# First stage of a transformer-block kernel: tokens, modulation quarters and weight rows issued in another order

## The chip, the cores and the metric

The kernel runs on one core of a Trainium2 chip. The metric is device time in microseconds (us); before the change it was 843.18 us (median of three runs, 842.88 to 844.29). The granted TensorE clock was 0.998 to 1.00 in every run and every run was fast (none showed the lower clock and longer time that mark a slow run).

## The reference, cut to what matters

```python
mod = (silu(c) @ w_mod)                    # six rows of 1024: sa, ca, ga, sb, cb, gb
h = layernorm(x) * (1 + ca) + sa           # x: 2048 tokens x 1024
x = x + ga * linear_attention(h, wqkv, wo) # 32 heads, phi(t) = elu(t) + 1
h = layernorm(x) * (1 + cb) + sb
x = x + gb * (gelu(h @ w_gate) * (h @ w_up)) @ w_down   # 3584 wide
```

The first stage computes, for four blocks of 128 tokens (each called a token below, first to fourth), `h` and the products K = h @ wk and V = h @ wv. K sums over eight blocks `dc` of 128 rows of `wk`. The modulation `1 + ca`, `sa` comes in four quarters `q`: quarter q serves the K rows dc = 2q and 2q+1. So K rows can start as soon as their quarter and their weights are there.

## The kernel before: the parts that matter

Loads go out on one queue (`Q`, the SyncE queue) in this order:

```python
sch.dma(Q, ... C8[:], c_v)                 # c, eight rows, 2 KB
x_dma(0, 1); x_dma(1, 2); wmq_dma(0, (1,)) # tokens 1, 2; half of quarter 0
x_dma(2, 3); wmq_dma(0, (0,)); x_dma(3, 4)
w_dma(WK, ..., 0, 2)                       # wk rows dc 0,1
for q in range(1, 4):
    wmq_dma(q)                             # quarter q, two loads of 512 KB
    w_dma(WK, ..., 2 * q, 2 * q + 2)       # wk rows dc 2q, 2q+1, 512 KB
w_dma(WV, ..., 0, 512)                     # wv, left half of its columns, 1 MB
w_dma(WV, ..., 512, 1024)
```

In the timelines of this stage each engine starts its instructions in the order of the program, so the order of the lines below matters. `warm(n)` issues n filler matmuls, whose results nobody reads, to keep TensorE busy. `ln1_bn`, `ln1_fin`, `xhat_dve` are the layer norm on VectorE (DVE); `t1` transposes a token on TensorE and copies it out on ScalarE (ACT); `mod_cols` makes the columns of a quarter on TensorE, `mod_copy` and `mod1` apply them on DVE; `k_part(q, tokens)` are the K matmuls of quarter q. Seven of the eight K results (4 tokens x 2 halves) stay in seven banks of PSUM (the memory that TensorE writes its results to) through all quarters; the eighth needs bank 4, which holds the modulation columns, so it can only run after the last quarter.

```python
warm(12, 7)
ln1_bn(0, 0); ln1_bn(0, 1); ln1_fin(0); ln1_bn(1, 0); xhat_dve(0, ...); t1(0, 5)
warm(7, 7)
ln1_bn(1, 1); ln1_fin(1); ln1_bn(2, 0); xhat_dve(1, ...); t1(1, 6)
warm(1, 7); mod_cols(0, 4, False); warm(6, 7)
ln1_bn(2, 1); ln1_fin(2); ln1_bn(3, 0); xhat_dve(2, ...)
mod_copy(0, 4); mod1(0, 2, 0, 2); t1(2, 7)
ln1_bn(3, 1); ln1_fin(3); mod1(2, 1, 0, 2)
k_part(0, [0, 1]); xhat_dve(3, ...); k_part(0, [2]); t1(3, 7)
mod_cols(1, 4); mod1(0, 3, 2, 4); mod1(3, 1, 0, 4)
warm(3); k_part(1, [0, 1, 2])
mod_cols(2, 4); mod1(0, 4, 4, 6)
k_part(0, [3]); k_part(1, [3]); warm(1)
k_part(2, [0, 1, 2])                       # "third rows of K"
mod_cols(3, 4); mod1(0, 4, 6, 8)
k_part(2, [3]); warm(2)
k_part(3, [0, 1, 2, 3])                    # for dc: for bank
... k_evac of seven banks ...
kv_mm(3, "k", 1, 4, list(range(NDC)))      # the eighth result, all eight rows
k_evac(3, 1, 4)
for c_ in range(4):
    for jg in range(2):                    # left half of wv, then right half
        kv_mm(c_, "v", jg, nb(), ...); v_evac(...)
    ...
```

Of the kernel before, what the change touches and what calls it, by code (L numbers as in the profile page):

```python
# [12 lines left out]
D = 1024  # L13
# [4 lines left out]
NDC = D // P  # L18
# [27 lines left out]
OFF_WK = OFF_WD  # L46
OFF_WV = OFF_WD + 16384
# [167 lines left out]
def bass_adaLN_cond__linear_attn_block__geglu_ffn__prompt_kernel(  # L215
# [15 lines left out]
    with ExitStack() as es:  # L231
# [79 lines left out]
        def r_sm(name):  # L311
            return [(SMO[name], SMO[name] + SMSZ[name], name)]
# [78 lines left out]
        sch = Sched()  # L391
# [34 lines left out]
            gop(lambda e, k=k: e.memset(bm32f[32 * k:32 * (k + 1), 8 * k:8 * k + 33 * 7 + 1:33], 1.0), wr=r_sm("bm32"))  # L426


        sch.dma(Q, lambda e: e.dma_start(C8[:], c_v), wr=r_sm("c8"), note="c8")

        def x_dma(c0, c1):
            return sch.dma(Q, lambda e: e.dma_start(XALL[:, c0:c1, :], x_v[:, c0:c1, :]), wr=r_xs(c0, c1), note=f"x{c0}")
# [4 lines left out]
        def w_dma(dst, off, name, kind, c0, c1, dc0=0, dc1=NDC):  # L437
            return sch.dma(Q, lambda e: e.dma_start(dst[:, dc0:dc1, c0:c1], wqkv_v[:, dc0:dc1, kind * D + c0:kind * D + c1]),
                           wr=[t_ for dc in range(dc0, dc1) for t_ in r_w(off, name, dc, c0, c1)], note=f"{name}.{dc0}.{c0}")
# [15 lines left out]
        w_dma(WK, OFF_WK, "wk", 1, 0, D, 0, 2)  # L455
        for q in range(1, 4):
            wmq_dma(q)
            w_dma(WK, OFF_WK, "wk", 1, 0, D, 2 * q, 2 * q + 2)
        w_dma(WV, OFF_WV, "wv", 2, 0, 512)
        w_dma(WV, OFF_WV, "wv", 2, 512, 1024)  # L460
        x_dma(4, 8)
        w_dma(WQ, OFF_WQ, "wq", 0, 0, 512)
# [30 lines left out]
        def xhat_dve(c_, dst, rng):  # L493
            sch.op(V, lambda e: e.tensor_scalar(dst[:, :], XALL[:, c_, :], MVA[:, c_, 0:1], RSA[:, c_:c_ + 1],
                                                op0=ALU.subtract, op1=ALU.mult),
                   rd=r_x(c_) + r_smc("mv", c_, 8) + r_smc("rs", c_, 4), wr=rng, note=f"xhat {c_}")
# [5 lines left out]
        def xh_buf(c_):  # L502
            i = c_ % 3
            return XH[i], r_2k(XHO[i], f"xh{i}")
# [10 lines left out]
        def t1(c_, tb):  # L515
            b_, rng = xh_buf(c_)
            sg, ci = divmod(c_, CPG)
            for dc in range(NDC):
                sch.op(T, lambda e, dc=dc: e.transpose(PS16(tb, dc * P, (dc + 1) * P), b_[:, dc * P:(dc + 1) * P], IDENT[:, :]),  # L519
                       rd=rng + r_sm("ident"), pwr=pr(tb), note=f"T1 {c_}.{dc}")  # L520
            sch.op(A, lambda e: e.activation(H1[sg][:, :, ci * P:(ci + 1) * P], PS16(tb).rearrange("p (a b) -> p a b", a=NDC), ACTF.Copy),
                   prd=pr(tb), wr=r_h1(sg, 0, NDC, ci * P, (ci + 1) * P), note=f"h1raw {c_}")
# [26 lines left out]
        def mod1(c0, n, dc0=0, dc1=NDC):  # L549
            sg, ci = divmod(c0, CPG)  # L550
            mods(H1, r_h1, sg, sc1, ci * P, (ci + n) * P, dc0, dc1, "h1")
# [6 lines left out]
        def mod_cols(q, bank, copy=True):  # L558
            o = None
            rng = [(bank * 2048 + q * 16, bank * 2048 + (q + 1) * 16)]  # L560
            for t in range(2):
                for b in range(2):
                    col = q * 4 + t * 2 + b
                    for dc in range(NDC):
                        o = sch.op(T, lambda e, t=t, b=b, dc=dc, col=col: e.matmul(  # L565
                            PS(bank, col, col + 1), WMQ[q][:, dc, t, b * P:(b + 1) * P], SILUT[:, dc:dc + 1],
                            start=(dc == 0), stop=(dc == NDC - 1)),
                            rd=r_wmq(q, t) + r_sm("siluT"), pwr=(rng if dc == 0 else ()), note=f"mod{q}.{t}.{b}.{dc}")
            for t_ in rng:
                sch.ps.set_writer(t_[0], t_[1], o)  # L570
            if copy:
                mod_copy(q, bank)

        def mod_copy(q, bank):
            rng = [(bank * 2048 + q * 16, bank * 2048 + (q + 1) * 16)]
            sch.op(V, lambda e: e.tensor_tensor(MODT[:, q * 4:q * 4 + 4], PS(bank, q * 4, q * 4 + 4), ADD4[:, :], ALU.add),
                   prd=rng, rd=r_sm("add4"), wr=r_smc("modt", q, 16), note=f"modcp{q}")
# [29 lines left out]
        def kv_mm(c_, kind, jg, bank, dcs):  # L607
            sg, ci = divmod(c_, CPG)
            W_, off, name = (WK, OFF_WK, "wk") if kind == "k" else (WV, OFF_WV, "wv")
            o = None  # L610
            for dc in dcs:
                o = sch.op(T, lambda e, dc=dc: e.matmul(PS(bank), H1[sg][:, dc, ci * P:(ci + 1) * P], W_[:, dc, jg * 512:(jg + 1) * 512],  # L612
                                                        start=(dc == 0), stop=(dc == NDC - 1)),
                           rd=r_h1(sg, dc, dc + 1, ci * P, (ci + 1) * P) + r_w(off, name, dc, jg * 512, (jg + 1) * 512),
                           pwr=(pr(bank) if dc == 0 else ()), note=f"{kind} c{c_} jg{jg} dc{dc}")
            if dcs[-1] == NDC - 1:
                pset_writer(bank, o)
# [5 lines left out]
        def v_evac(c_, jg, bank):  # L623
            i = c_ % 3
            sch.op(A, lambda e: e.activation(VS[i][:, jg * 4:jg * 4 + 4, 0:P], PS(bank).rearrange("p (a b) -> p a b", a=4), ACTF.Copy),
                   prd=pr(bank), wr=r_vs(i, jg * 4, jg * 4 + 4, 0, P), note=f"vcp{c_}.{jg}")
# [39 lines left out]
        def warm(n, bank=None):  # L666
            for _ in range(n):
                sch.op(T, lambda e: e.matmul(PS(0 if bank is None else bank), WARM[:, 0:P], WARM[:, :], start=bank is not None,  # L668
                                             stop=bank is not None, skip_group_check=True),
                       rd=R_WARM, pwr=pr(bank) if bank is not None else (), note="warm")  # L670

        def ln1_bn(c_, h):
            src = XALL[:, c_, h * 512:(h + 1) * 512]
            sch.op(V, lambda e: e.bn_stats(STA[:, c_, h * 6:h * 6 + 6], src), rd=r_x(c_, h * 512, h * 512 + 512), wr=r_smc("st", 2 * c_ + h, 24), note=f"bn{h} A{c_}")

        def ln1_fin(c_):
            sch.op(V, lambda e: e.bn_aggr(MVA[:, c_, :], STA[:, c_, :]), rd=r_smc("st", c_, 48), wr=r_smc("mv", c_, 8), note=f"aggr A{c_}")
            sch.op(V, lambda e: e.tensor_scalar(VEA[:, c_:c_ + 1], MVA[:, c_, 1:2], 1e-5, None, op0=ALU.add),
                   rd=r_smc("mv", c_, 8), wr=r_smc("ve", c_, 4), note=f"ve A{c_}")
            sch.op(G, lambda e: e.tensor_tensor(RSA[:, c_:c_ + 1], VEA[:, c_:c_ + 1], NEGHALF[:, :], ALU.pow),  # L680
                   rd=r_smc("ve", c_, 4) + r_sm("neghalf"), wr=r_smc("rs", c_, 4), deps=[last_g[0]], note=f"rstd A{c_}")

        kb0 = {(0, 0): 0, (0, 1): 1, (1, 0): 2, (1, 1): 3, (2, 0): 5, (2, 1): 6, (3, 0): 7}

        def k_part(q, cs):
            for dc in (2 * q, 2 * q + 1):
                for (c_, jg), b in kb0.items():
                    if c_ in cs:
                        kv_mm(c_, "k", jg, b, [dc])


        warm(12, 7)
        ln1_bn(0, 0)
        ln1_bn(0, 1)
        ln1_fin(0)
        ln1_bn(1, 0)
        xhat_dve(0, *xh_buf(0))
        t1(0, 5)
        warm(7, 7)
        ln1_bn(1, 1)  # L700
        ln1_fin(1)
        ln1_bn(2, 0)
        xhat_dve(1, *xh_buf(1))
        t1(1, 6)
        warm(1, 7)
        mod_cols(0, 4, False)
        warm(6, 7)
        ln1_bn(2, 1)
        ln1_fin(2)
        ln1_bn(3, 0)  # L710
        xhat_dve(2, *xh_buf(2))
        mod_copy(0, 4)
        mod1(0, 2, 0, 2)
        t1(2, 7)
        ln1_bn(3, 1)
        ln1_fin(3)
        mod1(2, 1, 0, 2)
        k_part(0, [0, 1])
        xhat_dve(3, *xh_buf(3))
        k_part(0, [2])  # L720
        t1(3, 7)
        mod_cols(1, 4)
        mod1(0, 3, 2, 4)
        mod1(3, 1, 0, 4)
        warm(3)
        k_part(1, [0, 1, 2])
        mod_cols(2, 4)
        mod1(0, 4, 4, 6)
        k_part(0, [3])
        k_part(1, [3])  # L730
        warm(1)
        k_part(2, [0, 1, 2])
        mod_cols(3, 4)
        mod1(0, 4, 6, 8)
        k_part(2, [3])
        warm(2)
        k_part(3, [0, 1, 2, 3])
        for (c_, jg), b in kb0.items():
            k_evac(c_, jg, b)
        kv_mm(3, "k", 1, 4, list(range(NDC)))  # L740
        k_evac(3, 1, 4)
        for c_ in range(4):
            for jg in range(2):
                b = nb()
                kv_mm(c_, "v", jg, b, list(range(NDC)))
                v_evac(c_, jg, b)
            if c_ == 0:
                ln1(4)
                for k, t in enumerate((4, 5, 10, 11)):
                    wm_dma(t, k)  # L750
            if c_ >= 1:
                kvacc(c_ - 1)
            if c_ == 1:
                ln1(5)
            if c_ == 2:
                ln1(6)
                x_dma(12, 16)
                t1d(6)
                t1(4, 4)
                mod1(4, 1)  # L760
# [389 lines left out]
```

## Time and profile before

| | before |
|---|---|
| median, range | 843.18 us, 842.88 to 844.29 (843.33 over six runs) |
| TensorE busy | 830.7 of 841.3 us |
| V starts | 31.40 us |
| first product of K with V starts | 38.56 us |
| first query matmul starts | 47.72 us |
| last landing mark of: first token, first quarter, third rows of wk, right half of wv | 3.90, 10.19, 22.27, 33.29 us |

Lines of the page: busy time per engine, busy share of the 16 DMA engines in 40 slices of 21 us (tenths), the DMA queues, and the chain of waits by engine.

```profile
...
PE 830.7 (99%) x4149; PEld 387.9 (46%) x4229; DVE 492.0 (58%) x883; ACT 294.9 (35%) x483; POOL 24.4 (3%) x64
...
DMA  9991824029778587340555533055553305555000
...
q8 instruction: 34, 0.56, 0.3%
...
PE 96%; DVE 2%; issue 1%; ACT 1%; DMA 0%; ACTq 0%
...
```

TensorE is busy for 99% of the span and holds 96% of the chain. But "busy" counts fillers and modelled ends. Only the first two slices can change, and there the DMA engines are also full ("99"). The useful question is therefore which of the two ended last, stage by stage.

How to read starts. In the timeline the first number is the start, the second the length of the merged group, and the form "128x512" tells its size. A matmul is shown 0.379 us long, but successive 512-wide matmuls start 0.216 us apart, so true idle time on TensorE is start-to-start minus 0.216. L668 is the filler, L565 the quarter columns, L612 K or V, L519 a transpose, L576 the copy of the columns, L538 the modulation. The timeline of before around its last quarter:

```profile
...
24.99 0.94 PE L565 MATMUL ps_all<-siluT,wmq 128*128 128x1 bf16 x32
...
25.79 0.59 PE L612 MATMUL ps_all<-wk,h1T 128*128 128x512 bf16 x2
25.97 0.16 DVE L576 TENSOR_TENSOR modt<-ps_all,add 128x4 f32<-128x4 f32 x1 [3.72 <-PE ps_all L565]
...
26.17 0.73 DVE L538 TENSOR_SCALAR h1T<-h1T,modt 128x512 bf16<-128x512 bf16 x2
26.22 0.59 PE L668 MATMUL ps_all<-warm 128*128 128x512 bf16 x2
...
26.87 4.70 PE L612 MATMUL ps_all<-wk,h1T 128*128 128x512 bf16 x21
...
31.40 2.79 PE L612 MATMUL ps_all<-wv,h1T 128*128 128x512 bf16 x11
...
```

The columns of the last quarter are issued from 24.99 to 25.79 us; the copy and modulation take DVE to 26.58 for the first row; TensorE meanwhile does two K matmuls and two fillers, and goes on at 26.87. V starts at 31.40. 24 useful matmuls take 24 x 0.216 = 5.18 us, but 25.79 to 31.40 is 5.61: 0.43 us are lost here.

The chain of waits of before in order of time (start, length, what) in the middle of the stage:

```profile
...
15.66 0.45 PE ps_all L519 x8
16.11 0.78 PE ps_all L565 x32
16.89 0.08 issue
16.96 0.59 PE ps_all L668 x2
...
17.56 2.76 PE ps_all L612 x12
20.32 0.38 PE ps_all L565 x16
20.70 0.02 issue
20.72 0.55 PE ps_all L565 x16
...
```

Columns of the second quarter at 16.11, fillers, K rows at 17.56; then the columns of the third quarter break at 20.70, where their second half lands (its last mark is 20.67), and the third rows of K start at 22.40, 0.13 us after the last mark of their weights (22.27).

**Landing marks.** A load raises its semaphore (the counter that its users wait on) 16 times; the trace holds the time of each, called a mark here (of c, eight rows, it shows 9). The Trainium skill ("DMA: Bandwidth & Descriptors", "Why a DMA increments its semaphore by 16 and not by 1") says that the engines finish independently and only the full 16 mean that all data has landed. The second load of the third quarter has its fourteenth mark at 19.55 us and its last at 20.67, and the columns went on after the last, at 20.72. In before the first quarter's fourteenth mark is at 9.09 us, its last at 10.19: stragglers of 1.10 us will matter below.

### The profile page before, as it was taken

The numbers are of one execution on the slowest core, as the hardware profiler recorded it, in microseconds if no ns is written. First come the engines' busy times: TensorE is split into PE (matmuls) and PEld (weight loads), VectorE is DVE, ScalarE is ACT, GpSimd is POOL, SyncE is SP. The second block draws the span as 40 slices with busy tenths as digits, with TensorE's granted clock in tenths as the row PEclk, the third lists the DMA queues.
The fourth block names the chain that finished last, engine by engine and source line by source line (L and its number), as shares of the span: only waits on it lengthen the run. The fifth ranks groups of instructions, "written<-read, shape, count | busy, mean of one in ns | idle before, by whom it ended". The sixth has DMA issues, their size and how long they took to land.

```text
span 841.3 us, 11255 instructions
## 1 busy us (share of the span) xinstructions
PE 830.7 (99%) x4149; PEld 387.9 (46%) x4229; DVE 492.0 (58%) x883; ACT 294.9 (35%) x483; POOL 24.4 (3%) x64
## 2 busy tenths in 40 slices
PE   8999999999999999999999999999999999999998
PEld 4454444444444444444444444444444444444445
DVE  5666767867785555654455665346666535655522
ACT  2343333335513344420355442044444104445300
POOL 2000000000200000010000001000000000000000
PEclk9999999999999999999999999999999999999999
DMA  9991824029778587340555533055553305555000
GB/s 286 354 285 26 263 47 105 14 54 233 165 165 252 155 253 206 105 97 23 149 153 154 153 102 69 26 157 150 150 151 101 75 19 158 152 157 141 7 19 26
DMA packets 181750, 112.70 MB, mean 134 GB/s; under 512 B 33080, under 2 KB 172728, under 8 KB 180672
## 3 DMA queue, kind: packets, MB, share of 16 engines
q1 hardware_dynamic: 181696, 111.98, 49.0%
q8 instruction: 34, 0.56, 0.3%
q14 instruction: 20, 0.16, 0.1%
HBM read 100.67 MB, written 4.47 MB: 125 GB/s over the span
## 4 chain that ended last, share of the span: by engine, by line
PE 96%; DVE 2%; issue 1%; ACT 1%; DMA 0%; ACTq 0%
PE ps_all L1006 23%; PE ps_all L1031 23%; PE ps_all L1003 22%; PE ps_all L612 12%; PE ps_all L934 7%; PE ps_all L653 6%; PE ps_all L668 1%; PE ps_all L634 1%; DVE h1T L538 1%; PE ps_all L584 0%; PE ps_all L836 0%; PE ps_all L565 0%; PE ps_all L519 0%; DVE ww L1019 0%; DVE ww L1016 0%
## 5 line engine op out<-in xcount | busy, mean ns | idle before, releaser
L1006 PE MATMUL ps_all<-h2T,wu 128*128 128x512 bf16 x896 | 339.6, 379 | 2.0
L1003 PE MATMUL ps_all<-h2T,wg 128*128 128x512 bf16 x859 | 325.6, 379 | 0.0
L1031 PE MATMUL ps_all<-wd,yT 128*128 128x512 bf16 (+1 forms) x907 | 193.2, 372 | 0.9
L1014 ACT ACTIVATE q<-ps_all 128x512 f32<-128x512 f32 x112 | 66.9, 597 | 229.4 <-PE ps_all L1003 224.5
L1031 PEld LDWEIGHTS ps_all<-wd,yT 128*128 128x128 bf16 x924 | 90.4, 98 | 103.2
L1003 PEld LDWEIGHTS ps_all<-h2T,wg 128*128 128x128 bf16 x896 | 87.7, 98 | 105.8 <-issue 0.2
L1006 PEld LDWEIGHTS ps_all<-h2T,wu 128*128 128x128 bf16 x896 | 87.7, 98 | 105.6
L1016 DVE SCALAR_TENSOR_TENSOR ww<-q,ps_all 128x512 f32<-128x512 f32 x112 | 77.0, 688 | 88.2 <-ACT guh L1015 88.2
L1019 DVE SCALAR_TENSOR_TENSOR ww<-th,guh 128x512 f32<-128x512 f32 x112 | 77.6, 693 | 77.9 <-ACT th L1018 77.9
L1018 ACT ACTIVATE th<-ww 128x512 f32<-128x512 f32 x112 | 70.5, 630 | 85.8 <-DVE ww L1016 85.8
L1021 DVE TENSOR_TENSOR yT<-ww,ps_all 128x512 bf16<-128x512 f32 x112 | 76.9, 687 | 3.8
L1036 DVE TENSOR_TENSOR ps_all<-ps_all,gbb 128x512 f32<-128x512 f32 (+1 forms) x33 | 22.5, 683 | 94.8 <-PE ps_all L1031 94.8
L1015 ACT ACTIVATE guh<-ps_all 128x512 f32<-128x512 f32 x112 | 66.3, 592 | 0.0
L601 ACT ACTIVATE eb<-ps_all 128x512 f32<-128x512 f32 x64 | 37.5, 601 | 77.9 <-PE ps_all L612 37.8
L653 PE MATMUL ps_all<-h1T,wq 128*128 128x512 bf16 x245 | 56.8, 379 | 1.4 <-DVE pq L604 0.7
L612 PE MATMUL ps_all<-wv,h1T 128*128 128x512 bf16 x254 | 57.8, 379 | 0.2
L612 PE MATMUL ps_all<-wk,h1T 128*128 128x512 bf16 x251 | 57.6, 379 | 0.2
L934 PE MATMUL ps_all<-w,pq 128*128 128x512 bf16 x251 | 56.0, 379 | 0.3
L602 DVE TENSOR_SCALAR eb<-eb 128x512 f32<-128x512 f32 x64 | 27.1, 424 | 34.0 <-ACT eb L601 33.6
L934 PEld LDWEIGHTS ps_all<-w,pq 128*128 128x128 bf16 x256 | 25.0, 98 | 30.2 <-issue 0.2
L612 PEld LDWEIGHTS ps_all<-wv,h1T 128*128 128x128 bf16 x256 | 24.9, 98 | 30.0 <-DVE eb L602 0.6
L612 PEld LDWEIGHTS ps_all<-wk,h1T 128*128 128x128 bf16 x256 | 24.6, 98 | 29.8 <-DVE h1T L538 1.5
(81 smaller groups left out, 398.8 us busy)
## 6 DMA issues: line engine op xcount, KB each, us to landing
wg<-in_B_w_gate_dram SPq DMA_DIRECT2D x56, 512.0 KB, 4.1
wu<-in_B_w_up_dram SPq DMA_DIRECT2D x56, 512.0 KB, 5.3
wmst<-in_w_mod_dram SPq DMA_DIRECT2D x8, 1024.0 KB, 11.6
rb<-scr_rd SPq DMA_DIRECT2D x32, 256.0 KB, 6.9
wd<-in_B_w_down_dram SPq DMA_DIRECT2D x7, 1024.0 KB, 7.6
wmq<-in_w_mod_dram SPq DMA_DIRECT2D x8, 512.0 KB, 7.0
out_dram<-xall SPq DMA_DIRECT2D x31, 128.0 KB, 1.7
xall<-in_A_x_dram SPq DMA_DIRECT2D x3, 1024.0 KB, 11.9
```

The lines of the kernel that those rows point to most:

```text
L612: o = sch.op(T, lambda e, dc=dc: e.matmul(PS(bank), H1[sg][:, dc, ci * P:(ci + 1) * P], W_[:, dc, jg * 512:(jg + 1) * 512], start=(dc == 0 ...
L653: o = sch.op(T, lambda e, dc=dc: e.matmul(PS(b), WQ[:, dc, qc * P:(qc + 1) * P], H1[sg][:, dc, :], start=(dc == 0), stop=(dc == NDC - 1)), ...
L934: last[half] = sch.op(T, lambda e, g=g, half=half: e.matmul(PS(b0 + half), PQ[sg][:, g, ci * P:(ci + 1) * P], W2[:, g, half * 512:(half + ...
L1003: og = sch.op(T, lambda e, dc=dc: e.matmul(PS(bg), WG[slot][:, dc, e_ * P:(e_ + 1) * P], H2[sg][:, dc, :], start=(dc == 0), stop=(dc == ND ...
L1006: ou = sch.op(T, lambda e, dc=dc: e.matmul(PS(bu), WU[slot][:, dc, e_ * P:(e_ + 1) * P], H2[sg][:, dc, :], start=(dc == 0), stop=(dc == ND ...
L1014: sch.op(A, lambda e: e.activation(Q1[j][:, :], PS(bg), ACTF.Square, scale=math.sqrt(GELU_A)), prd=pr(bg), wr=rq, note=f"q1 {fc}")
L1015: ogh = sch.op(A, lambda e: e.activation(GUH[j][:, :], PS(bg), ACTF.Copy, scale=0.5), prd=pr(bg), wr=rg, note=f"gh {fc}")
L1016: sch.op(V, lambda e: e.scalar_tensor_tensor(WW[j][:, :], Q1[j][:, :], 1.0, PS(bg), op0=ALU.add, op1=ALU.mult), rd=rq, prd=pr(bg), wr=rw, ...
L1018: sch.op(A, lambda e: e.activation(TH[j][:, :], WW[j][:, :], ACTF.Tanh, scale=GELU_C), rd=rw, wr=rt, note=f"th {fc}")
L1019: sch.op(V, lambda e: e.scalar_tensor_tensor(WW[j][:, :], TH[j][:, :], 1.0, GUH[j][:, :], op0=ALU.add, op1=ALU.mult), rd=rt + rg, wr=rw, n ...
L1021: sch.op(V, lambda e: e.tensor_tensor(YT[:, fc, :], WW[j][:, :], PS(bu), ALU.mult), rd=rw, prd=pr(bu), wr=r_yt(fc), note=f"yT {fc}")
L1031: o = sch.op(T, lambda e, b=b, fc=fc, c0=c0, c1=c1, n=n: e.matmul(PS(b, 0, n), YT[:, fc, ci * P:(ci + 1) * P], WDT[fc // 4][:, fc % 4, c0:c1],
```

## The change

Its intent: start the loads sooner, apply each quarter and token as it arrives, fill the wait at the last quarter, and let V use the left half of its weights for two tokens before the right half is needed.

```diff
-        sch.dma(Q, lambda e: e.dma_start(C8[:], c_v), wr=r_sm("c8"), note="c8")
+        sch.dma(A, lambda e: e.dma_start(C8[:], c_v), wr=r_sm("c8"), note="c8")
 ...     # last wk rows in two loads, left half of wv in two loads
-        w_dma(WV, OFF_WV, "wv", 2, 0, 512)
+            for d0, d1 in ((2 * q, 2 * q + 2),) if q < 3 else ((6, 7), (7, 8)):
+                w_dma(WK, OFF_WK, "wk", 1, 0, D, d0, d1)
+        w_dma(WV, OFF_WV, "wv", 2, 0, 512, 0, 4)
+        w_dma(WV, OFF_WV, "wv", 2, 0, 512, 4, 8)
 ...     # front, as it stands after the change (cut):
+        warm(11, 7)
+        ... t1(0, 5) ... warm(6, 7)
+        mod_cols(0, 4, False)
+        ln1_bn(2, 0); xhat_dve(1, ...); t1(1, 6); ln1_bn(2, 1); ln1_fin(2)
+        mod_copy(0, 4); mod1(0, 1, 0, 2)
+        warm(4, 7); k_part(0, [0])
+        ln1_bn(3, 0); mod1(1, 1, 0, 2); k_part(0, [1])
+        xhat_dve(2, ...); t1(2, 7); ln1_bn(3, 1); ln1_fin(3)
+        mod1(2, 1, 0, 2); warm(5); k_part(0, [2])
+        xhat_dve(3, ...); mod_cols(1, 4); mod1(0, 3, 2, 4); t1(3, 7)
+        k_part(1, [0, 1, 2]); mod1(3, 1, 0, 4); k_part(0, [3])
+        mod_cols(2, 4); mod1(0, 4, 4, 6); k_part(1, [3]); warm(1)
         k_part(2, [0, 1, 2]); mod_cols(3, 4); mod1(0, 4, 6, 8); k_part(2, [3])
-        warm(2)
-        k_part(3, [0, 1, 2, 3])
+        kv_mm(3, "k", 1, 4, list(range(6)))
+        for (c_, jg), b in kb0.items():
+            kv_mm(c_, "k", jg, b, [6, 7])
+        kv_mm(3, "k", 1, 4, [6, 7])
 ...
-            for jg in range(2):
+            for vc, jg in (((0, 0), (1, 0)), ((0, 1), (1, 1)), ((2, 0), (2, 1)), ((3, 0), (3, 1)))[c_]:
```

Four parts: **c** (its load moves to the ScalarE queue), **front** (order up to the last quarter), **tail** (six rows of the eighth result fill the wait), **V** (left half split, V order changed).

More of the change, by code (lines that the diff above doesn't have):

```diff
@@ L457, in bass_adaLN_cond__linear_attn_block__geglu_ffn__prompt_kernel @@
             wmq_dma(q)
-            w_dma(WK, OFF_WK, "wk", 1, 0, D, 2 * q, 2 * q + 2)
-        w_dma(WV, OFF_WV, "wv", 2, 0, 512)
+            for d0, d1 in ((2 * q, 2 * q + 2),) if q < 3 else ((6, 7), (7, 8)):
+                w_dma(WK, OFF_WK, "wk", 1, 0, D, d0, d1)
+        w_dma(WV, OFF_WV, "wv", 2, 0, 512, 0, 4)
+        w_dma(WV, OFF_WV, "wv", 2, 0, 512, 4, 8)
         w_dma(WV, OFF_WV, "wv", 2, 512, 1024)
@@ L683, in bass_adaLN_cond__linear_attn_block__geglu_ffn__prompt_kernel, with k_part @@
         kb0 = {(0, 0): 0, (0, 1): 1, (1, 0): 2, (1, 1): 3, (2, 0): 5, (2, 1): 6, (3, 0): 7}
-        def k_part(q, cs):
-            for dc in (2 * q, 2 * q + 1):
+        def k_part(q, cs, dcs=(0, 1)):
+            for dc in [2 * q + k for k in dcs]:
                 for (c_, jg), b in kb0.items():
@@ L689, in k_part @@
                         kv_mm(c_, "k", jg, b, [dc])
-        warm(12, 7)
+        warm(11, 7)
         ln1_bn(0, 0)
@@ L698, in bass_adaLN_cond__linear_attn_block__geglu_ffn__prompt_kernel @@
         t1(0, 5)
-        warm(7, 7)
         ln1_bn(1, 1)
         ln1_fin(1)
+        warm(6, 7)
+        mod_cols(0, 4, False)
         ln1_bn(2, 0)
@@ L704, in bass_adaLN_cond__linear_attn_block__geglu_ffn__prompt_kernel @@
         t1(1, 6)
-        warm(1, 7)
-        mod_cols(0, 4, False)
-        warm(6, 7)
         ln1_bn(2, 1)
         ln1_fin(2)
+        mod_copy(0, 4)
+        mod1(0, 1, 0, 2)
+        warm(4, 7)
+        k_part(0, [0])
         ln1_bn(3, 0)
+        mod1(1, 1, 0, 2)
+        k_part(0, [1])
         xhat_dve(2, *xh_buf(2))
-        mod_copy(0, 4)
-        mod1(0, 2, 0, 2)
         t1(2, 7)
@@ L717, in bass_adaLN_cond__linear_attn_block__geglu_ffn__prompt_kernel @@
         mod1(2, 1, 0, 2)
-        k_part(0, [0, 1])
+        warm(5)
+        k_part(0, [2])
         xhat_dve(3, *xh_buf(3))
-        k_part(0, [2])
-        t1(3, 7)
         mod_cols(1, 4)
         mod1(0, 3, 2, 4)
+        t1(3, 7)
+        k_part(1, [0, 1, 2])
         mod1(3, 1, 0, 4)
-        warm(3)
-        k_part(1, [0, 1, 2])
+        k_part(0, [3])
         mod_cols(2, 4)
         mod1(0, 4, 4, 6)
-        k_part(0, [3])
         k_part(1, [3])
@@ L735, in bass_adaLN_cond__linear_attn_block__geglu_ffn__prompt_kernel @@
         k_part(2, [3])
-        warm(2)
-        k_part(3, [0, 1, 2, 3])
+        kv_mm(3, "k", 1, 4, list(range(6)))
+        for (c_, jg), b in kb0.items():
+            kv_mm(c_, "k", jg, b, [6, 7])
+        kv_mm(3, "k", 1, 4, [6, 7])
         for (c_, jg), b in kb0.items():
             k_evac(c_, jg, b)
-        kv_mm(3, "k", 1, 4, list(range(NDC)))
         k_evac(3, 1, 4)
         for c_ in range(4):
-            for jg in range(2):
+            for vc, jg in (((0, 0), (1, 0)), ((0, 1), (1, 1)), ((2, 0), (2, 1)), ((3, 0), (3, 1)))[c_]:
                 b = nb()
-                kv_mm(c_, "v", jg, b, list(range(NDC)))
-                v_evac(c_, jg, b)
+                kv_mm(vc, "v", jg, b, list(range(NDC)))
+                v_evac(vc, jg, b)
             if c_ == 0:
```

## The prediction

> **What bounds the kernel.** TensorE. The page shows PE busy 830.7 of 841.3 us and the chain of waits 96% PE, at granted clock 1.00. From about 31 us on matmuls follow one another at 0.216 us in the timeline. The change touches only the first stage, so it can win only what TensorE wastes there. In the timeline the stage runs from 2.2 us to 31.40 us, where the V products start. It holds 64 K matmuls (13.8 us), four token transposes (about 2.2), four modulation quarters (3.2). The rest is filler ("warm") matmuls and short gaps: 12 fillers up to 7.41 us, 7 to 9.70, one at 10.15, 6 to 12.46, 3 near 17, one at 22, two at 26.2.
>
> **What paces it.** DMA: the windows view has its share at about 1.1 from 5 to 60 us. From the landing semaphores: first token 3.9, first quarter 7.7 and 10.2, K rows 12.25, 17.2, 22.3, 26.4, last quarter half 25.1, V halves 30.4 and 33.3. TensorE consumes the second and later quarters within 0.2 to 1 us of landing; the chain then goes quarter columns (0.80), copy (0.16), modulation of two rows (0.41 each), K.
>
> **What changes.**
> 1. c goes to the other DMA queue. The timeline has its issue at 0.72 to 1.13 us ahead of the first token's at 1.19, so all later loads should land 0.45 us earlier. The Trainium skill ("Trainium Kernel Development and Optimization", Key Constraints) says queues share the 16 engines and another issuer saves only issue time; that is what I count. One filler less (0.43 us, half clock) lets the first transposes start at 6.98.
> 2. Tail: before, the last quarter's columns end at 25.79, V starts at 31.40: 5.61 us for 24 K matmuls (5.18), hence 0.43 us wasted. Six K rows of the eighth bank now fill that wait: gain 0.43.
> 3. Front: the first quarter now precedes the second token's transposes. It waits for its load (10.2-0.45 = 9.75), so: columns to 10.65, transposes to 11.1, copy to h1T (1.02) to 12.3, modulation to 12.9, third token's normalisation to 13.35, transposes to 14.13, h1T 15.35, modulation, K rows of the third token 15.75 to 16.6, second quarter's columns 16.6 to 17.4 (before: 15.95 to 16.75). Then K 18.2, third quarter 21.2 (20.16), K third rows 22.9 (22.40), last quarter 25.5 (24.99), V at 31.45 (31.40). These are estimates from durations in the timeline. So the serial ACT/DVE chain of the third token gives back what 1 and 2 gain.
> 4. V split and reordered: removes a gap of about 0.1 us at 33.3 us, where the second V half's landing bound.
> After 48 us nothing changes; a shift of the V start passes through one to one, because there TensorE is the limit.
>
> **Predicted time:** 843.0 us, range 841.8 to 844.0. Faster by over 2%: 0.01; within 2%: 0.98; slower: 0.01.
>
> **What would show it.** First token's statistics start at 3.45 (before 3.92): step 1. No filler and no gap between the last quarter's columns and V: step 2. Second quarter's columns start at 16.3 to 16.9, later than before in spite of earlier loads: step 3. V at 31.1 to 31.7; all groups after 48 us unchanged in number and mean duration.
>
> **What would make it wrong.** If the third token's chain is shorter than I add up, the second quarter starts at its landing (15.4) and V up to 0.6 us sooner. If the gaps of about 0.5 us (before the first quarter, before the third token's K) let the clock fall back: the skill's "TensorE: Matmul & The Clock Gate", Part 1, ties full clock to recent activity; the trace shows 0.427 us per matmul until 8.1 us, 0.216 after. Gaps of 0.2 us did no harm before; a fall would cost microseconds. Run-to-run spread of before (842.88 to 844.29) exceeds the effect.

## The result and the profile after

842.83 us median (842.44 to 843.81, six runs) against 843.33 us (842.88 to 844.29, six runs). The ratio, computed here and below as the mean time of one kernel's fast runs over that of the other's of the same rounds (so not quite the ratio of the medians), is 0.9994 with a 95% interval of 0.9981 to 1.0007: within 2%, and not told from zero.

The same lines of the page after:

```profile
...
PE 834.0 (99%) x4224; PEld 387.2 (46%) x4224; DVE 492.5 (59%) x885; ACT 294.8 (35%) x483; POOL 24.8 (3%) x64
...
DMA  9991833029878587330555533055553305555000
...
q10 hardware_dynamic: 16, 0.00, 0.0%
...
PE 99%; DVE 1%; issue 0%; POOL 0%; ACT 0%; POOLq 0%
...
```

There is a new queue, q10, with the 16 packets of c. The count of matmuls is higher only because the trace of before misses some records (859 of the 896 gate products, for one). Shares say little here; the stage marks tell more:

| mark, us | before | after | change |
|---|---|---|---|
| last mark of first token / first quarter | 3.90 / 10.19 | 3.48 / 9.06 | -0.42 / -1.13 |
| second quarter's columns start | 15.95 | 15.94 | 0.0 |
| third rows of wk, last mark | 22.27 | 21.67 | -0.60 |
| third rows of K start | 22.40 | 22.24 | -0.16 |
| V starts | 31.40 | 30.82 | -0.58 |
| first product of K with V | 38.56 | 37.73 | -0.83 |
| end of the span | 841.26 | 840.49 | -0.77 |

The span after the first query matmul is 793.4 to 793.8 us in all fourteen traces, so all that differs lies before 48 us. The 0.77 us of this pair is one execution each; the medians differ by 0.50.

The timeline after around the last quarter (L567 columns, L614 K and V):

```profile
...
24.84 0.94 PE L567 MATMUL ps_all<-siluT,wmq 128*128 128x1 bf16 x32
...
25.64 5.34 PE L614 MATMUL ps_all<-wk,h1T 128*128 128x512 bf16 x24
25.82 0.16 DVE L578 TENSOR_TENSOR modt<-ps_all,add 128x4 f32<-128x4 f32 x1 [3.31 <-PE ps_all L567]
26.02 0.73 DVE L540 TENSOR_SCALAR h1T<-h1T,modt 128x512 bf16<-128x512 bf16 x2
...
30.82 7.07 PE L614 MATMUL ps_all<-wv,h1T 128*128 128x512 bf16 x32
...
```

From the end of the column issue (25.64) K runs without a break to V at 30.82: 5.18 us instead of 5.61. The chain of waits after, in order of time:

```profile
...
11.39 1.77 PE ps_all L614 x8
13.16 0.46 PE ps_all L521 x8
13.62 0.02 issue
13.64 1.03 ACT h1T L523
14.67 0.03 issue
14.70 0.32 DVE h1T L540
15.02 0.05 issue
15.07 1.04 PE ps_all L614 x4
16.11 0.79 PE ps_all L567 x32
...
```

New in it are "ACT h1T" (1.03 us, the copy of the third token) and "DVE h1T" (its modulation): TensorE now stands waiting for the third token before the K rows at 15.07, and the columns of the second quarter follow only at 15.94, although their load has been complete since 14.71.

### The profile page after: what moved, and what is told of

Read it like the earlier page. It is cut to its first block, busy times and chain, and to the rows that moved or that the text cites. A ratio compares the mean times of both kernels' runs of the same rounds, so it can differ in the third digit from the quotient of the medians.

```text
span 840.5 us, 11330 instructions
## 1 busy us (share of the span) xinstructions
PE 834.0 (99%) x4224; PEld 387.2 (46%) x4224; DVE 492.5 (59%) x885; ACT 294.8 (35%) x483; POOL 24.8 (3%) x64
## 4 chain that ended last, share of the span: by engine, by line
PE 99%; DVE 1%; issue 0%; POOL 0%; ACT 0%; POOLq 0%
PE ps_all L1035 23%; PE ps_all L1010 23%; PE ps_all L1007 23%; PE ps_all L614 13%; PE ps_all L938 7%; PE ps_all L655 6%; PE ps_all L636 1%; PE ps_all L670 1%; PE ps_all L586 0%; PE ps_all L840 0%; PE ps_all L567 0%; PE ps_all L521 0%; PE ps_all L852 0%; DVE kvbd L827 0%; ACT h1T L523 0%
## 5 line engine op out<-in xcount | busy, mean ns | idle before, releaser
L1007 PE MATMUL ps_all<-h2T,wg 128*128 128x512 bf16 x896 | 339.6, 379 | 0.0
L1040 DVE TENSOR_TENSOR ps_all<-ps_all,gbb 128x512 f32<-128x512 f32 (+1 forms) x33 | 22.5, 682 | 94.8 <-PE ps_all L1035 94.8
L655 PE MATMUL ps_all<-h1T,wq 128*128 128x512 bf16 x256 | 58.7, 379 | 0.7 <-DVE pq L606 0.7
L614 PE MATMUL ps_all<-wk,h1T 128*128 128x512 bf16 x256 | 58.2, 379 | 0.6 <-DVE h1T L540 0.6
L614 PE MATMUL ps_all<-wv,h1T 128*128 128x512 bf16 x256 | 57.7, 379 | 0.0
L604 DVE TENSOR_SCALAR eb<-eb 128x512 f32<-128x512 f32 x64 | 27.1, 424 | 33.6 <-ACT eb L603 33.3
L614 PEld LDWEIGHTS ps_all<-wv,h1T 128*128 128x128 bf16 x256 | 25.0, 98 | 29.7
L614 PEld LDWEIGHTS ps_all<-wk,h1T 128*128 128x128 bf16 x256 | 24.5, 98 | 30.7 <-DVE h1T L540 2.3
```

The lines of the kernel that those rows point to most:

```text
L614: o = sch.op(T, lambda e, dc=dc: e.matmul(PS(bank), H1[sg][:, dc, ci * P:(ci + 1) * P], W_[:, dc, jg * 512:(jg + 1) * 512], start=(dc == 0 ...
L655: o = sch.op(T, lambda e, dc=dc: e.matmul(PS(b), WQ[:, dc, qc * P:(qc + 1) * P], H1[sg][:, dc, :], start=(dc == 0), stop=(dc == NDC - 1)), ...
L1007: og = sch.op(T, lambda e, dc=dc: e.matmul(PS(bg), WG[slot][:, dc, e_ * P:(e_ + 1) * P], H2[sg][:, dc, :], start=(dc == 0), stop=(dc == ND ...
```

## Experiments

All outputs were correct. Kernels of a call share a chip and the runs of before.

| run | what | median (range), n | before, same call | ratio, 95% interval |
|---|---|---|---|---|
| b_again | before | 843.07 (842.55 to 844.11), 4 | 843.12 | 0.9997 (0.9984 to 1.0009) |
| a_again | changed kernel | 842.43 (842.28 to 843.10), 5 | 843.12 | 0.9989 (0.9978 to 1.0001) |
| b_c8act | before + c | 842.55 (842.18 to 844.67), 6 | 843.12 | 0.9994 (0.9982 to 1.0007) |
| a_c8sp | changed without c | 843.26 (843.04 to 845.50), 6 | 843.12 | 1.0002 (0.9991 to 1.0014) |
| a_front_old | changed without front | 842.26 (841.77 to 843.45), 5 | 842.98 | 0.9991 (0.9978 to 1.0005) |
| a_cols2 | changed, one move | 842.72 (842.22 to 843.06), 5 | 842.98 | 0.9995 (0.9982 to 1.0007) |
| b_tail | before + tail | 843.21 (842.63 to 843.59), 5 | 842.98 | 1.0000 (0.9987 to 1.0013) |
| b_v | before + V | 843.91 (842.71 to 844.37), 5 | 842.98 | 1.0007 (0.9994 to 1.0019) |
| a_third | changed kernel | 843.32 (842.78 to 843.45), 5 | 843.25 | 0.9999 (0.9986 to 1.0011) |
| a_front_old2 | changed without front | 842.53 (842.02 to 842.58), 5 | 843.25 | 0.9989 (0.9976 to 1.0001) |
| best | that + wk split | 842.58 (841.85 to 842.88), 5 | 843.25 | 0.9989 (0.9977 to 1.0002) |
| b_tail_v | before + tail + V | 842.52 (842.20 to 842.76), 5 | 843.25 | 0.9991 (0.9977 to 1.0005) |

Marks of the profiled execution of each kernel (us), read from the traces: last mark of the third rows of wk; start of the third rows of K, and how long after that mark; V start and its distance from the third rows; from V to the first product of K with V.

| trace | weights land | K rows start (after) | V starts (after) | V to K-V product |
|---|---|---|---|---|
| before | 22.27 | 22.40 (0.13) | 31.40 (9.00) | 7.16 |
| b_again | 23.11 | 23.25 (0.14) | 32.42 (9.17) | 6.97 |
| b_c8act | 22.05 | 22.18 (0.13) | 31.18 (9.00) | 6.91 |
| b_v | 22.46 | 22.69 (0.23) | 32.90 (10.21) | 6.90 |
| b_tail | 22.30 | 22.48 (0.18) | 31.05 (8.57) | 7.58 |
| b_tail_v | 22.16 | 22.37 (0.21) | 30.94 (8.57) | 6.90 |
| a_front_old | 22.17 | 22.42 (0.25) | 30.99 (8.57) | 6.90 |
| a_front_old2 | 22.26 | 22.47 (0.21) | 31.04 (8.57) | 6.91 |
| best | 21.38 / 22.07 | 21.52 (0.14) | 30.58 (9.06) | 6.91 |
| after | 21.67 | 22.24 (0.57) | 30.82 (8.58) | 6.91 |
| a_again | 21.90 | 22.33 (0.43) | 30.91 (8.58) | 6.90 |
| a_third | 22.57 | 22.70 (0.13) | 31.27 (8.57) | 7.62 |
| a_c8sp | 22.91 | 23.05 (0.14) | 31.62 (8.57) | 6.90 |
| a_cols2 | 22.88 | 23.02 (0.14) | 31.58 (8.56) | 6.91 |

My theory: front gives back what c and tail gain, because it holds K by the third token's chain over ACT and DVE. Rivals: the move of c alone is the gain; the front order is part of the gain; the pair of traces differed by chance.

### The same two kernels again

> The kernel before, unchanged: a second look at its profile. In the first trace two of the 16 landing marks of the first quarter's half load came 1.0 and 1.2 us after the other fourteen, and kept that lag to 19 us. Theory (the lag is a cost of putting c, a transfer of eight rows, at the head of the same queue): the lag is there again, first quarter complete at 10.0 to 10.3 us. Rival (chance of one execution): the lag is gone or of another size, first quarter complete near 9.3. Either way V starts at 31.2 to 31.6 us and the ratio to before is 1.000 within 0.001.

> The changed kernel, unchanged: a second look. V starts at 30.8 within 0.3 us and the first query matmul at 46.9 (before 47.7) if the 0.8 us read from the first pair of traces is a property of the kernel; V at 31.2 or later if that pair differed by chance. Ratio 0.999, interval about 0.001 wide each way. First quarter complete at 9.1 us if the early landing is the kernel's, near 9.7 if chance.

The straggler lag of the first quarter in before came again (fourteenth mark 9.19, last 10.56 us), but V started at 32.42 instead of 31.40: its loads were late (third rows of wk at 23.11), and its own run took 844.11 us. So the statement that V starts at 31.2 to 31.6 either way missed: one kernel's V start moves by 1 us between executions, with its loads. The changed kernel gave V at 30.91, near the first, as forecast. "Lag is a cost of c in front" fell with the next two runs: b_c8act, with c moved, lagged 0.84 us, and a_c8sp, with c in front, only 0.25.

### c alone, and all but c

```diff
# b_c8act, on the kernel before
-        sch.dma(Q, lambda e: e.dma_start(C8[:], c_v), ...)
+        sch.dma(A, lambda e: e.dma_start(C8[:], c_v), ...)
# a_c8sp, on the changed kernel
-        sch.dma(A, lambda e: e.dma_start(C8[:], c_v), ...)
+        sch.dma(Q, lambda e: e.dma_start(C8[:], c_v), ...)
```

> The kernel before with only the load of c moved to the other queue. Theory (waits after the first quarter are set by the chain over ACT and DVE and by the fillers, and the tail waste of 0.43 us stays): loads land 0.45 us sooner or more, first transposes still at 7.3 to 7.4 because 12 fillers are kept, second quarter's columns at 15.4 to 16.0, K third rows at 21.8 to 22.4, V at 30.8 to 31.4: gain 0 to 0.6 us. Rival (the load of c alone explains the whole gain): V at 30.8 and first query matmul at 46.9.

> The changed kernel with the load of c put back at the head of the first queue. Theory: loads land 0.45 to 1.1 us later, the first quarter at 9.7 to 10.2 instead of 9.06, and the serial chain behind it passes that on: second quarter's columns at 16.5 to 17.0 us, third rows of K at 22.8 to 23.3, V at 31.4 to 31.9, so 0 to 0.5 us later than the kernel before at that mark; the V part then still wins 0.2. Total 843.0 to 843.8. Rival (front order itself is what gains): V still at 30.8 to 31.0.

b_c8act: medians 0.57 us below before, as much as the whole change; the marks agree with the theory (V at 31.18, tail still 9.00 - 8.57 = 0.43 us longer). One miss: its first transposes came at 6.48, not at 7.3 to 7.4: its fillers change from 0.427 to 0.216 us apart at 5.1 us, those of before at 8.1. The Trainium skill ("TensorE: Matmul & The Clock Gate", Part 1) says that the window in which activity is counted runs freely and the cold count differs from run to run; these traces agree, those of one kernel too: the fillers of the changed kernel change at 5.5 us in a_again and are still 0.427 apart at 6.4 us in after. a_c8sp: its third rows, its V start and its time came as forecast; its median is 0.14 us above before and 0.83 above a_again of the same call. Front, tail and V together gain nothing without c here; that tail and V do gain without c and without front is seen in b_tail_v below. Every interval contains 1, so single ratios prove nothing. The rival "c alone is the gain" is not refuted by times; the marks show that it isn't so: b_c8act still loses 0.43 us in the tail.

Over all 14 traces, the mean last mark with c in front (6 traces) against c moved (8) is 3.94 and 3.53 us for the first token, 10.29 and 9.41 for the first quarter, 22.5 and 22.2 for the third rows of wk. The move buys 0.4 us at first, as its issue time says; stragglers then add to or take from it.

### Tail alone, V alone, and both

```diff
# b_tail: the tail hunk of the change on the kernel before
# b_v: the WV load and V order hunks on the kernel before
# b_tail_v: both
```

> The kernel before with the tail alone changed: six K rows of the eighth bank in the wait for the last quarter, last rows bank by bank. Theory: from the end of the last quarter's columns to V 5.18 us (24 matmuls) instead of 5.61, in any execution where the last K weights have landed 2 us after those columns; the total 0.4 us below before, 842.6 to 842.9. Rival (the wait only moves: V then waits for its own weights, which land at 30.4): 5.6 us as before, no gain.

> The kernel before with the V part alone changed: the load of the first half of V in two pieces, V products of two tokens on the first half before the second half is used. Theory: V starts as before at 31.2 to 31.7 (later only if loads are late), from V to the first KV product 6.91 us always, where before took 6.97 to 7.16 when the second half landed after 33.2; total 0 to 0.25 us below before. Rival (it is a real part of the gain): 0.4 us or more below before.

> The kernel before with tail and V part changed together, c and front as before. Alone, the tail moved V from 31.40 to 31.05 us and then lost 0.67 us at the second half of V (landing 33.36), and the V part alone had nothing to win. Theory (they need each other): V 8.57 us after the third rows of K, 6.91 us from V to the first KV product, and the total 0.3 to 0.6 us below before, 842.4 to 842.8. Rival (only the moved load of c counts): no gain, 843.0 or more.

The tail did what was costed (8.57 instead of 9.00), and gained nothing: median 843.21 against 842.98. The timeline of b_tail shows where it went (L612 is V here; in brackets the idle time before and its releaser as the profile infers it):

```profile
...
31.05 1.89 PE L612 MATMUL ps_all<-wv,h1T 128*128 128x512 bf16 x8
...
33.42 2.50 PEld L612 LDWEIGHTS ps_all<-wv,h1T 128*128 128x128 bf16 x13 [0.98 <-DVE pk L604]
33.45 2.75 PE L612 MATMUL ps_all<-wv,h1T 128*128 128x512 bf16 x12 [0.51 <-DVE pk L604]
...
```

V starts at 31.05, and after eight matmuls TensorE stands until 33.45. The bracket names DVE, but the evacuation that frees this product's bank (the second of L604) had ended at 31.07; the last mark of the right half of wv is 33.36, 0.09 us before the restart. A wait for several semaphores is put down to one of them; the landing mark decides. The tail's gain was 0.43 us and this gap is 0.67 us (33.45 - 32.56 - 0.216), so it was more than given back: V to K-V product took 7.58 us. V alone gained nothing either: its median of 843.91 is 0.93 above before, where 0 to 0.25 below was forecast, a miss in time. Its profiled execution is the slowest of its five; the last rows of wk landed at 28.02 us there and V came at 32.90, which no V order can mend. From V to the product it took 6.90, as forecast. Why its other runs were slow is not known. Both together: V to product 6.90 with no gap, median 842.52, and all five runs (up to 842.76) below all nine of before (from 842.92). The forecast for both (842.4 to 842.8) held. So the two parts need each other: the tail brings V forward into a load that is not there, and the V order supplies 1.73 us of other work. My forecast for b_tail (a gain of 0.4 in time) was a miss; its mark was right.

### Front undone

```diff
# a_front_old, on the changed kernel: from warm(11, 7) to the last quarter the order of before,
# with 11 instead of 12 fillers at the start; c, tail and V as in the change
```

> The changed kernel (load of c on the other queue, V split, tail filled) with the order of the kernel before up to the last quarter, with 11 fillers at the start. Theory (the new front order is what gives back the gain: it pins the third rows of K at 22.24 us by a chain over ACT and DVE even when their weights have landed): third rows of K start when their weights are in, at 21.4 to 21.9 us, V starts 8.6 us after that, 30.0 to 30.5, and the median is 0.3 to 0.6 us below the changed kernel's, 842.0 to 842.4. If the weights of the third rows land late (22.2 or more), V at that plus 8.7. Rival (the new front order is part of the gain): third rows at 22.3 or later with weights landed by 21.8, V at 30.9 or later, median 843.0 or more.

> The changed kernel a third time, beside the next three on the same chip. Theory: third rows of K at the later of 22.2 us (its own chain) and 0.13 us after their last landing mark; V 8.57 us after that; median 842.4 to 842.9. A third rows start before 22.1 would refute the pin by the new front order.

> The changed kernel with the old front order, unchanged from its first run, where the median was 842.26 and the lowest 841.77. Theory: again 0.2 to 0.5 us below the changed kernel of this call in median and in the lowest run, since nothing but loads holds its third rows of K; they start 0.1 to 0.3 us after the last landing mark, and before 22.1 us if that is before 21.8. Rival (the first difference was chance): the two medians within 0.1 us or the other way round.

a_front_old had 842.26 us, a_front_old2 842.53, both beside a before of 843 or so; a_third, the changed kernel in the second's call, 843.32. In that call all five runs of a_front_old2 (up to 842.58) lie below all five of a_third (from 842.78); means 842.38 and 843.20. The forecasts for this call (0.2 to 0.5 apart, a_third at 842.4 to 842.9) were both missed: the difference was 0.79 and a_third's median 843.32. Means of all runs: before 843.31 (39 runs), changed 842.92 (16), front undone 842.40 (10). Against the before of its own call, the changed kernel's median was 0.50 and 0.69 below and 0.07 above; the front undone was 0.72 below twice. The marks I had forecast for the front undone (K rows at 21.4 to 21.9, V at 30.0 to 30.5) were not seen in the two profiled executions: the loads landed at 22.17 and 22.26, and V at 30.99 and 31.04 is no earlier than after and a_again. What was seen is what holds TensorE. The clearest measure is the time from the columns of the first quarter to those of the second, here before (L565) and after (L567):

```profile
10.37 0.94 PE L565 MATMUL ps_all<-siluT,wmq 128*128 128x1 bf16 x32
...
15.95 0.94 PE L565 MATMUL ps_all<-siluT,wmq 128*128 128x1 bf16 x32
```

```profile
9.11 0.94 PE L567 MATMUL ps_all<-siluT,wmq 128*128 128x1 bf16 x32
...
15.94 0.94 PE L567 MATMUL ps_all<-siluT,wmq 128*128 128x1 bf16 x32
```

It is 5.58 us in all nine traces with the old front and 6.81 to 6.87 in all five with the new one, whatever the loads did: the new front makes this stretch 1.25 us longer. In those five the second quarter's columns start 1.2 us after their load; with the front undone (15.24 and 15.36) it is 0.36 and 0.21 us. Whether that reaches V depends on the next load. Chain of waits of a_front_old2, in order of time:

```profile
...
12.08 8.85 DMA wmq<-in_w_mod_dram
...
20.98 0.55 PE ps_all L567 x16
21.53 0.89 PE ps_all L614 x4
22.41 0.22 PE ps_all L670
22.63 2.59 PE ps_all L614 x12
25.22 0.78 PE ps_all L567 x32
26.00 5.20 PE ps_all L614 x24
```

The chain goes into a load: the third quarter waited for its last mark (20.93), and everything after that is TensorE without a gap to V. Compare the chain after, where ACT and DVE stand in it. The column "after" in the table of marks says the same: with the old front the third rows start 0.13 to 0.25 us after their weights in every trace (where it is 0.18 or more, the load of the third quarter ended last: K rows start 1.54 to 1.56 us after its last mark in all five); with the new front and weights early (21.67, 21.90) they wait 0.57 and 0.43 us for their own chain; with weights late (22.57 and later) the chain does not show.

Why a_third was slow: its chain of waits, in order of time, has two loads in it, one of them hidden under "issue":

```profile
...
13.64 8.93 DMA wk<-in_A_wqkv_dram
22.57 0.14 issue
22.70 2.75 PE ps_all L614 x12
...
26.23 8.66 PE ps_all L614 x40
34.88 0.55 issue
35.44 3.61 PE ps_all L614 x16
```

K waits for weights to 22.57 (third rows). The second, 0.55 us of "issue" in modelled ends, is 0.71 us of true idle time (35.44 - 34.51 - 0.216); the right half of wv has its fourteenth mark at 32.83 and its last at 35.34. So of the 0.94 us between the spans of the profiled executions of a_third and a_front_old2, 0.71 us is stragglers, not order; V itself starts only 0.23 us later (31.27 and 31.04). Whether the other runs of a_third had the same is not known. That the front order delays the second quarter is shown in all five traces with it; that it also holds the third rows of K, in two (after and a_again), by 0.44 and 0.30 us beyond the 0.13 that K needs after a landing. Not all of that is the front's: the third quarter landed at 20.33 and 20.56 there, and with the 1.54 us that the old front needs after it, K would have started at 21.87 and 22.10, so an estimated 0.37 and 0.23 us remain. How much of the times it makes is left open: the medians of the one shared call differ by 0.79 us, the means of all runs by 0.5; and a_c8sp, which differs from b_tail_v in the front (and in a split of the last wk rows and one filler), was 0.14 above its before where b_tail_v was 0.73 below, but in another call.

### One move in the new front

```diff
# a_cols2, on the changed kernel
         k_part(1, [0, 1, 2]); mod1(3, 1, 0, 4)
-        k_part(0, [3])
         mod_cols(2, 4); mod1(0, 4, 4, 6)
+        k_part(0, [3])
         k_part(1, [3])
-        warm(1)
```

> The changed kernel with one move: the fourth token's first K rows (two matmuls) come after the third quarter's columns instead of before them, and the one filler there is dropped. Theory: the third quarter's columns start 0.43 us sooner (20.16) and, once its load (20.3 us) is in, the third rows of K start at 21.8 instead of 22.24, if their weights have landed; V at 30.4, total 0.3 to 0.45 us below the changed kernel. Rival (loads, not that chain, set the third rows): third rows still at 22.2, no gain.

Inconclusive. The move did what it was costed for: from the second quarter's columns to the third's it took 4.22 us (16.66 to 20.87) instead of 4.65 (15.94 to 20.59 in after). But the load of the third quarter ended at 21.52 and that of the K rows at 22.88 us in the profiled execution, so the chain that the move shortens was not the limit. Median 842.72, lowest 842.22, as the changed kernel in its other calls; it was not run beside it.

### An attempt to beat both

```diff
# best, on a_front_old
-            for d0, d1 in ((2 * q, 2 * q + 2),) if q < 3 else ((6, 7), (7, 8)):
+            for d0, d1 in ((2, 4),) if q == 1 else ((2 * q, 2 * q + 1), (2 * q + 1, 2 * q + 2)):
-        k_part(1, [3]); warm(1)
+        k_part(1, [3])
```

> The version before this one, with the third pair of K rows loaded in two pieces and the filler ahead of their products dropped: an attempt to beat both kernels. Theory: its third rows wait for the first of the two pieces only, which lands 0.7 us before the second; then the modulation of the third quarter (its load, columns, copy) is the next limit, so at most 0.1 to 0.3 us sooner; median 841.8 to 842.3. Rival (one more descriptor set or the missing filler costs as much): equal to the version before this one.

Its third rows started at 21.52, the earliest of all, on the first of the two pieces (21.38); TensorE had then stood 0.48 us for it, and stood 0.48 us more in the last quarter's columns for their load (24.95). V at 30.58 is the earliest too, but the times equal those of the version before it (842.58 and 842.53), so the forecast of 841.8 to 842.3 was missed: the wait has moved to the next load. The changed kernel with the old front has the most runs at this level: 10, mean 842.40, 0.11% below before (842.40 / 843.31), though each interval by itself still touches 1. b_tail_v, which does not move c, had the same median in the call that they share (842.52 and 842.53): once tail and V are in and the front is the old one, these runs show no further gain from c (nor from the split of the last wk rows and the filler less that go with it).

### What moves the loads

The DMA table of the page has a queue of instruction fetches (q8). In the traces its packets are 16 KB; two fall into the first stage, where they take 0.95 to 1.22 us and begin at 16.5 to 18.9 and at 27.6 to 31.1 us. In a_third the first began at 17.35 and took 1.21 us: the lag from the fourteenth to the last landing mark is 0.05 us in the load that ended at 16.42 and 1.43 us in the next one (18.20 and 19.63). The second fetch began at 31.13, and the right half of wv lagged by 2.51 us. a_c8sp shows the same step (0.25 to 1.75 us after a fetch at 17.55), and so do six others after their first fetch: after (0.03 to 0.81), a_again (0.49 to 1.21), a_cols2 (0.08 to 1.58), a_front_old (0.34 to 1.10), a_front_old2 (0.25 to 1.09) and best (0.04 to 1.07). In before, where two marks lagged already, a third joins them: the load that ended at 22.27 has its last four marks at 20.90, 21.79, 21.98 and 22.27. The trace does not tell which engine carries a packet, so that the fetch delays its engine's share of the loads is inferred from the time and the size of the step. The lag that before, b_again and b_v have from the first quarter on (1.10, 1.37, 1.35 us) begins before any such fetch; its cause stays open.

## Why the prediction was right or wrong

- **Total: right.** 843.0 predicted, 842.83 measured, range 841.8 to 844.0. It forecast a change of 0.2 us and the medians differ by 0.5, both within the noise. There is luck in it: the range of 2.2 us would have held with no change at all, and two of the marks named as tests missed (below).
- **What bounds the kernel: right.** Everything behind the first query matmul took the same time (793.4 to 793.8 us).
- **Step 1, loads 0.45 us earlier: the mis-sized term.** The first token came 0.42 earlier, the first transposes at 6.91 (6.98 predicted). But the first quarter, taken as 9.75, landed at 9.06: in the one trace of before it had 1.10 us of stragglers, in the one of after 0.07. I took a landing that varies by execution as a constant of the kernel.
- **Step 3, the serial chain of the new front: right in mechanism, shifted by that term.** From the first quarter's columns (9.11) to the second's (15.94) it took 6.83 us, 6.75 predicted. With 9.06 in place of 9.75 every mark of the estimate falls in place, after the fact: 15.91 (15.94 measured), 17.5 (17.56), 22.2 (22.24), 30.8 (30.82). The other four traces with this front agree with the chain (6.81 to 6.87 us). The test "second quarter's columns at 16.3 to 16.9" and "V at 31.1 to 31.7" failed by the same 0.6 to 0.7 us.
- **Step 2, tail 0.43 us: right in size**, in all traces with it (8.56 to 8.58 us from the third rows to V instead of 9.00; 9.06 in best, with 0.48 us of waiting for the last quarter in it). Not foreseen: alone it is lost at the right half of wv.
- **Step 4, V gap 0.1 us: too small.** I read 0.10 us off the chain of waits, which runs on modelled ends; start to start the gap was 0.474 - 0.216 = 0.26 us, and V to the first product fell from 7.16 to 6.91.
- **"Gives back what 1 and 2 gain": partly.** The front gave back step 1 (second quarter's columns at the same 15.94 in spite of earlier loads), not step 2.
- **The clock did not fall**, the risk named there: start-to-start gaps of 0.77 us (after, a_again) and up to 1.43 us (b_v, before its last K rows) were followed by matmuls 0.216 us apart, against 0.427 at the start.

## What to carry to other kernels

When two resources are both full, a faster piece in one only helps if the next load is there: cost each gain together with the landing that comes next, as tail and V show (no gain each, 0.7 us in the medians together). Take the landing of a load from several executions, by its last mark, not from one trace. And a reorder by arrival should be checked for serial chains over other engines that it puts in front of work whose data comes early (1.25 us here).

## What the Trainium skill lacked or had wrong

- "Runtime: NRT & Kernel Launch", section "Instruction fetch mechanics", calls the cost of crossing a 16 KiB block of instructions one tail bump, mostly hidden. The runs agree on the block (34 packets of 16,384 bytes on q8) but show a packet of up to 1.22 us, after which the last landing mark of loads in flight lagged by 1.43 and 1.75 us in two traces (a_third, a_c8sp) instead of 0.05 and 0.25, with steps of 0.7 to 1.5 us in six more; no page says that loads can be held up this way. The link is inferred from timing.
- "DMA: Bandwidth & Descriptors" says that engines finish independently, but no page gives a size of the spread (it calls two of the engines usually slower in traces, without a figure): here the fourteenth and the sixteenth mark of the load that completes the first quarter were 0.05 to 1.37 us apart, and differed between executions of one kernel (0.07, 0.59 and 0.05 in the changed one); V of before started at 31.40 and 32.42 us in two executions, each time after its late last marks.
- Nothing wrong here, but tested: "Trainium Kernel Development and Optimization", Key Constraints, says that issuing from several engines saves only issue time. The runs agree: issue of the first token at 0.72 instead of 1.19 us, its last mark 0.41 us earlier in the mean.
